# Transposing q and k three loop iterations ahead of their tiles instead of four, with later fills and loads of v

## The chip, the cores and the metric

The kernel runs on one core of a Trainium2 chip. The core has five engines with queues of their own: TensorE (PE, matmuls and transposes), VectorE (DVE), ScalarE (ACT), GpSimd (POOL) and SyncE (SP, which here only issues DMAs). Each engine works through its instructions in order, and waits for others by semaphores. The metric is the time of one execution in microseconds (us).

## What is computed

The program chains three layers; N = 4608 tokens of 512 features come out of the first.

```
scores = scale * q_c @ k_c^T                 # per head and chunk of 64 tokens; B=8, H=8, S=576, D=64
attn   = exp(scores - max) / (sum + 1e-9)
x      = attn @ v_c                          # -> [4608, 512]
e      = argmax(x @ w_gate)                  # one of 8 experts per token
x      = p_e * relu(x @ w1[e]) @ w2[e]       # p_e: the softmax weight of that expert
out    = relu(x @ w_in)**2 @ w_out
```

## The kernel before

The work runs in three stages on the same core: `attention()`, `experts()` and `second()`. The order of the instructions on each engine is the order in which the Python code emits them. Only `attention()` and what stands around it is touched.

Attention works on tiles of 128 tokens (36 tiles, two chunks of 64 each) and loads q and k in units of two tiles (18 units, 512 KB each for q and for k). One loop iteration `it` does, in this order: POOL's `regroup` (L269), a copy of the q or k of a later unit into `by_r`; the `scores` of tile it+1 (PE L311), with DVE's maximum and subtraction (L319, L321); `pv` of tile it-1 (PE L344) with DVE's division (L353 to L356), a store of x, and now and then the load of a later batch's v on POOL's queue (L260); the transposition `ta` of tile it's attention weights (PE L332, copied out by ACT as `aT`, L334); the first half of a transposition of q or k (`trans`, PE L294); `x_t`, a transposition of an older tile's x (PE L371, copied out by DVE L372); the exponential of tile it+1 (ACT L326); and the second half of `trans`. Every fourth iteration the router's steps are added (`gate`, `gate_route`, `place`, `scatter`).

`trans` writes two kinds of buffers. For q, ACT copies each half into `qT` (L297). For k, ACT copies each half, in two pieces, into one of the two buffers `kb` (L302), which hold k in a form with zeros between, filled once at the start (`fill_k`). q and k alternate from iteration to iteration, so a unit takes two iterations: in the kernel before, q of unit u is transposed in iteration 2u-4, k in 2u-3, and the first scores of that unit are emitted in iteration 2u-1:

```
u, h2 = divmod(it + 4, 2)
tr = it + 4 < NTILE
if it + 6 < NTILE:
    regroup(it + 6)
```

For the first unit there is no regroup: PE transposes straight from the loaded tile, in 64-row pieces, and ACT copies them out (L288). v lies in two sets of four buffers `vb`, one set for batches 0, 2, .. and one for 1, 3, ..; around the loaded values stand zeros and a column of ones, written once (`fill_v`). Before the loop, POOL issues half of batch 0's v, fills all four buffers of batch 1 and issues the loads of batch 1; DVE fills those of batch 0 inside iteration -3.

At the end of attention, POOL has two more kinds of work: `scatter`, which writes the tokens' places to memory, and parts of the weights' splitting into two halves (L190, behind an ACT cast, L189). The experts' first tokens are gathered by POOL after the last of these scatters. The gathered tokens are transposed on PE and the first expert matmul (L780) follows.

Of the kernel before, what the change touches and what calls it, by code (L numbers as in the profile page):

```python
# [20 lines left out]
def kernel(ctx, tc, q, k, v, w_gate, w1, w2, w_in, w_out, out):  # L21
    nc = tc.nc
# [4 lines left out]
    NCB = S // CH  # L27
    NPAIR = H // 2
    KD = DM // 128
    NTILE = NT // 128  # L30
# [44 lines left out]
    def tl(tag, shape, dt, name):  # L75
        if tag in fixed:
            ts, n = fixed[tag]
            fixed[tag] = ts, n + 1
            t = ts[n % len(ts)].bitcast(dt)
            k = 1  # L80
            for z in shape[1:]:
                k *= z
            t = t[0:shape[0], 0:k]
            names = "abcde"[:len(shape) - 1]
            return t.rearrange(f"p ({' '.join(names)}) -> p {' '.join(names)}", **dict(zip(names, shape[1:])))
        if tag == "m":

            t = sb.tile([128, 32], F32, tag=tag, name=name, bufs=NBUF[tag]).bitcast(dt)
            names = "abc"[:len(shape) - 1]
            n = 1  # L90
            for z in shape[1:]:
                n *= z
            return t[0:shape[0], 0:n].rearrange(f"p ({' '.join(names)}) -> p {' '.join(names)}", **dict(zip(names, shape[1:])))
        return sb.tile(shape, dt, tag=tag, name=name, bufs=NBUF[tag])
# [134 lines left out]
    def attention():  # L229
        with ExitStack() as actx:  # L230
# [4 lines left out]
            vb = [[tl("hhhhhhba"[4 * s + p], [128, NCB, 2, D + 1], F32, f"vb{s}{p}") for p in range(NPAIR)] for s in range(2)]  # L235
# [5 lines left out]
            def load_qk(u):  # L241
                qk = tl("a", [128, 2, H, 2 * D], F32, f"qk{u}")
                for j, (src, nm) in enumerate(((q, "q"), (k, "k"))):
                    t = qk[:, j]
                    g = 4 * u
                    done = 0
                    while done < 4:
                        b, c = divmod(g + done, NCB)
                        n = min(4 - done, NCB - c)
                        nc.sync.dma_start(  # L250
                            out=t[32 * done:32 * (done + n)],
                            in_=src[b, :, c * CH:(c + n) * CH, :].rearrange("h (p r) d -> p h (r d)", r=2),
                        )
                        done += n
                    st[nm, u] = t

            def load_v(b, engs=(nc.gpsimd,), c0=0, c1=NCB):
                for p in range(NPAIR):
                    for j in range(2):
                        engs[j % len(engs)].dma_start(  # L260
                            out=vb[b % 2][p][64 * j:64 * j + 64, c0:c1, j, 0:D],
                            in_=v[b, 2 * p + j, CH * c0:CH * c1].rearrange("(c s) d -> s c d", s=CH),
                        )

            def regroup(z):
                u, j = divmod(z, 2)
                if u:
                    src = st["qk"[j], u].rearrange("p h (r d) -> p r h d", r=2)
                    nc.gpsimd.tensor_copy(out=by_r[:, z % 4], in_=src)  # L269

            def trans(nm, u, hh):
                if hh == 0:
                    if nm == "q":
                        st["qT", u] = tl("b", [128, NPAIR, 128, 2], F32, f"qT{u}")
                src = st[nm, u] if hh == 0 else st.pop((nm, u))
                ps = ps_t.tile([128, 2, 2, 128], F32, tag="t", name="tq")
                if u == 0:
                    for h in range(4):
                        nc.tensor.transpose(ps[:, h // 2, h % 2, :], src[:, 4 * hh + h, :], ident)
                    for r in range(2):  # L280
                        for j in range(2):
                            i_ = ps[64 * r:64 * r + 64, :, j, :]
                            if nm == "q":
                                o = st["qT", u][64 * j:64 * j + 64, 2 * hh:2 * hh + 2, :, r]
                            else:
                                i_ = i_.rearrange("p a (c i) -> p a c i", c=4)
                                o = kb[u % 2].rearrange("p a c j (i r) -> p a j c i r", r=2)[64 * j:64 * j + 64, 2 * hh:2 * hh + 2, j, :, :, r]
                            nc.scalar.copy(o, i_)  # L288
                    return
                z = 2 * u + (nm == "k")  # L290
                for a in range(2):
                    for r in range(2):
                        h = 4 * hh + 2 * a
                        nc.tensor.transpose(ps[:, a, r, :], by_r[:, z % 4, r, h:h + 2, :].rearrange("p h d -> p (h d)"), ident)  # L294
                i_ = ps.rearrange("p a r i -> p a i r")
                if nm == "q":
                    nc.scalar.copy(st["qT", u][:, 2 * hh:2 * hh + 2], i_)  # L297
                else:
                    o = kb[u % 2].rearrange("p a c j (i r) -> p j a c i r", r=2)
                    i_ = i_.rearrange("p a (c i) r -> p a c i r", c=4)  # L300
                    for j in range(2):
                        nc.scalar.copy(o[64 * j:64 * j + 64, j, 2 * hh:2 * hh + 2], i_[64 * j:64 * j + 64])  # L302
# [21 lines left out]
            def expo(i):  # L324
                at = st["at", i]
                nc.scalar.activation(out=at, in_=at, func=AF.Exp, scale=scale)  # L326

            def attn_t(i):
                at = st.pop(("at", i))
                ps = ps_t.tile([128, NPAIR, 128], F32, tag="t", name="ta")  # L330
                for p in range(NPAIR):
                    nc.tensor.transpose(ps[:, p, :], at[:, 2 * p:2 * p + 2, :], ident)  # L332
                aT = tl("r", [128, NPAIR, 128], F32, "aT")
                nc.scalar.copy(aT, ps)  # L334
                st["aT", i] = aT
# [60 lines left out]
            def fill_k(s):  # L396
                t = kb[s]
                nc.vector.memset(t[0:64, :, :, 1, :], 0.0)
                nc.vector.memset(t[64:128, :, :, 0, :], 0.0)

            def fill_v(s, eng):
                for t in vb[s]:
                    eng.memset(t[0:64, :, 1, :], 0.0)
                    eng.memset(t[64:128, :, 0, :], 0.0)
                    eng.memset(t[0:64, :, 0, D:D + 1], 1.0)
                    eng.memset(t[64:128, :, 1, D:D + 1], 1.0)

            fill_k(0)
            load_qk(1)
            c = min(6, NCB)  # L410
            load_v(0, (nc.gpsimd, nc.sync), 0, c)
            load_qk(2)
            if c < NCB:
                load_v(0, (nc.gpsimd, nc.sync), c)
            fill_v(1, nc.gpsimd)
            load_v(1)

            todo = {}
            for i in range(NTILE - 2):
# [6 lines left out]
            for g in range(NG - 1):  # L426
                t = 4 * g + (7 if g < NG - 3 else 6)
# [9 lines left out]
                    gather_tk(0)  # L437
                    gather(0)

            for it in range(-4, NTILE + 1):  # L440
                u, h2 = divmod(it + 4, 2)
                tr = it + 4 < NTILE
                if it + 6 < NTILE:
                    regroup(it + 6)
                if 0 <= it + 1 < NTILE:
                    scores(it + 1)
                if 0 <= it - 1 < NTILE:
                    pv(it - 1)
                    lo, hi = (2 * (it - 1)) // NCB, (2 * (it - 1) + 2) // NCB
                    if hi > lo and lo + 2 < B:  # L450
                        load_v(lo + 2)
                if 0 <= it < NTILE:
                    attn_t(it)
                if tr:
                    trans("qk"[h2], u, 0)
                for step, i in todo.get(it, ()):
                    step(i)
                if 0 <= it + 1 < NTILE:
                    expo(it + 1)
                if tr:  # L460
                    trans("qk"[h2], u, 1)
                    if h2 == 1 and u + 3 < NUNIT:
                        load_qk(u + 3)
                if it == -4:
                    fill_k(1)
                if it == -3:
                    fill_v(0, nc.vector)
                if it == -1:
                    constants()
                late_steps(it)  # L470
                if it == NTILE - 14:
                    for _ in range(4):
                        load_next(most=1)
                if NTILE - 5 <= it < NTILE - 2:
                    split(1, 0, it - NTILE + 5, eng=nc.gpsimd)
# [599 lines left out]
    with tc.manual_schedule():  # L1075
        attention()
        experts()
        second()
# [30 lines left out]
```

## Time and profile before

| | |
|---|---|
| median of 3 runs | 1463.49 us (1463.39 to 1469.42) |
| the profiled execution | 1463.5 us, of which the span from first to last instruction is 1461.7 us |
| PE busy | 1414.8 us (97%) |
| DVE busy | 766.7 us (52%) |
| ACT busy | 551.6 us (38%) |
| POOL busy | 502.5 us (34%) |
| mean granted PE clock | 0.991 of full speed |

The page lists each engine's busy time over the whole span. Attention is only the first eighth of it, so the stage is read from the busy time in short stretches and from the timeline. In the timeline a row is one instruction or several equal ones in a row (xcount): its start and length in us, the engine, the line of the code, and what it writes from what. In brackets stands how long the engine sat idle before, and who ended that wait.

### The profile page before, as it was taken

What the parts mean: (1) busy time and instruction counts of PE and PEld (TensorE: products, weight loads), DVE (VectorE), ACT (ScalarE), POOL (GpSimd) and SP (SyncE); (2) the same over time, 40 slices, a digit from 0 to 9 for tenths busy, and PEclk for the clock granted to TensorE, in tenths of its full rate; (3) what the DMA queues carried; (4) which work ended last, traced back from release to release, by engine and by line L of the source; (5) the groups of instructions that cost most, each with busy time, mean ns of one, the idle gap of its engine ahead of it and who ended that gap; (6) DMA issues with size and microseconds to landing.
All of it is one profiled execution on the core that took longest, in us unless ns stands there. A gap on an engine that the chain in (4) does not pass through costs nothing.

```text
span 1461.7 us, 21577 instructions
## 1 busy us (share of the span) xinstructions
PE 1414.8 (97%) x8186; PEld 1220.7 (84%) x8186; DVE 766.7 (52%) x1374; ACT 551.6 (38%) x941; POOL 502.5 (34%) x600
## 2 busy tenths in 40 slices
PE   5998889999999999999999999999999999999998
PEld 4887778888889999997888888888888888888886
DVE  4888877578888777884532223323322232232222
ACT  4665534344344446554432222222222222222222
POOL 6665754435555446743003040210404012040201
PEclk8999999999999999999999999999999999999999
DMA  9999546767677778884201010100101001010000
GB/s 206 266 219 255 166 143 188 211 195 231 208 240 234 221 234 262 265 271 155 73 6 55 1 60 0 38 23 1 60 0 60 0 22 38 1 60 0 31 2 29
DMA packets 144369, 172.90 MB, mean 118 GB/s; under 512 B 18160, under 2 KB 103872, under 8 KB 144256
## 3 DMA queue, kind: packets, MB, share of 16 engines
q1 hardware_dynamic: 110032, 112.58, 27.2%
q0 software_dynamic: 17920, 40.51, 9.7%
q10 hardware_dynamic: 16304, 18.36, 3.8%
q8 instruction: 66, 1.08, 0.3%
q14 instruction: 47, 0.39, 0.1%
HBM read 133.05 MB, written 38.34 MB: 117 GB/s over the span
## 4 chain that ended last, share of the span: by engine, by line
PE 54%; POOL 0%; POOLq 0%; issue 0%; DVE 0%
PE hp L1018 27%; PE py L1039 27%; POOL out_dram L999 0%; POOLq L1104 0%; DVE o L1047 0%; POOL between L998 0%
## 5 line engine op out<-in xcount | busy, mean ns | idle before, releaser
L1018 PE MATMUL hp<-xm,w_None 128*128 128x512 f32 x1728 | 416.7, 391 | 3.3 <-DVEq L962 3.3
L1018 PEld LDWEIGHTS hp<-xm,w_None 128*128 128x128 f32 x1728 | 325.5, 188 | 71.5 <-issue 3.5
L1039 PE MATMUL py<-w_None,h 128*128 128x512 f32 x1512 | 363.2, 389 | 0.0
L1039 PEld LDWEIGHTS py<-w_None,h 128*128 128x128 f32 x1512 | 283.9, 188 | 58.8
L1023 DVE SCALAR_TENSOR_TENSOR rs<-hp,rs 128x512 f32<-128x512 f32 x144 | 99.6, 692 | 434.1 <-ACT rs L1022 434.1
L1022 ACT ACTIVATE rs<-hp 128x512 f32<-128x512 f32 x144 | 86.0, 597 | 455.4 <-PE hp L1018 455.3
L999 POOL DMA_INDIRECT out_dram<-o,tp x36 | 35.1, 974 | 628.0 <-ACT o L1045 622.0
L780 PE MATMUL pa<-xs,w 128*128 128x256 f32 (+2 forms) x1344 | 243.8, 331 | 4.9 <-ACT xs L771 2.0
L792 PE MATMUL pb<-h,w 128*128 128x256 f32 (+2 forms) x1344 | 243.9, 331 | 0.0
L780 PEld LDWEIGHTS pa<-xs,w 128*128 128x128 f32 x1344 | 212.9, 191 | 22.6 <-DVE h L784 3.9
L792 PEld LDWEIGHTS pb<-h,w 128*128 128x128 f32 x1344 | 210.0, 190 | 14.4
L1025 DVE TENSOR_TENSOR h<-rs,h 128x512 fp32r<-128x512 f32 x144 | 99.8, 693 | 98.9 <-ACT h L1024 98.2
L190 DVE TENSOR_TENSOR w<-raw,w 128x1024 fp32r<-128x1024 f32 x100 | 134.0, 1341 | 17.2 <-ACT w L189 14.8
L783 ACT ACTIVATE h<-pa 128x256 fp32r<-128x256 f32 (+2 forms) x112 | 53.2, 475 | 219.1 <-PE pa L780 187.9
L1024 ACT CAST h<-rs 128x512 fp32r<-128x512 f32 x144 | 89.4, 621 | 111.5 <-DVE rs L1023 111.5
L189 ACT CAST w<-raw 128x1024 fp32r<-128x1024 f32 x113 | 118.1, 1046 | 0.0
L828 POOL TENSOR_TENSOR cr<-cr 128x256 f32<-128x256 f32 x64 | 49.5, 774 | 125.0 <-ACT h L783 48.0
L784 DVE SCALAR_TENSOR_TENSOR h<-pa,h 128x256 fp32r<-128x256 f32 (+2 forms) x112 | 59.6, 535 | 60.6 <-ACT h L783 57.2
L829 POOL TENSOR_TENSOR cr<-cr 128x256 f32<-128x256 f32 x64 | 73.7, 1151 | 5.0
L294 PE MATMUL tq<-ident,by_r 128*128 128x128 f32 x272 | 41.4, 279 | 14.0 <-POOL by_r L269 14.0
L223 POOL DMA_INDIRECT xg<-x_d,tk x40 | 44.6, 1116 | 28.0 <-PE pt L769 18.1
L1039 PE MATMUL py<-w,h 128*128 128x512 f32 x216 | 51.7, 389 | 0.0
(202 smaller groups left out, 1318.4 us busy)
## 6 DMA issues: line engine op xcount, KB each, us to landing
raw<-in_moe_w_dram SPq DMA_DIRECT2D x112, 512.0 KB, 4.1
x_d<-x SPq DMA_DIRECT2D x36, 256.0 KB, 6.2
x<-y_d POOLq DMA_DIRECT2D x36, 256.0 KB, 3.0
cr<-in_moe_w_in_dram SPq DMA_DIRECT2D x32, 256.0 KB, 4.2
cr<-in_moe_w_out_dram SPq DMA_DIRECT2D x32, 256.0 KB, 5.2
vb<-in_v_dram POOLq DMA_DIRECT2D x56, 144.0 KB, 8.0
qk<-in_q_dram SPq DMA_DIRECT2D x12, 512.0 KB, 8.6
qk<-in_k_dram SPq DMA_DIRECT2D x12, 512.0 KB, 10.7
```

Of the source, the lines that this page charges most:

```text
L189: nc.scalar.copy(w[0], raw)
L190: eng.tensor_tensor(out=w[1], in0=raw, in1=w[0], op=ALU.subtract)
L780: nc.tensor.matmul(ps[:, 0:N], lhsT=w[wl][:, kk, o:o + 128], rhs=xT[:, xl, kk, 0:N], start=(kk == 0 and wl + xl == 0), stop=(kk == KD - 1 ...
L784: nc.vector.scalar_tensor_tensor(out=h[:, 1, 0:N], in0=ps[:, 0:N], scalar=0.0, in1=h[:, 0, 0:N], op0=ALU.max, op1=ALU.subtract)
L792: nc.tensor.matmul(pb[d][:, 0:N], lhsT=w[wl][:, f % 2, 128 * d:128 * d + 128], rhs=h[:, hl, 0:N], start=(f + hl + wl == 0), stop=(f == NF ...
L829: nc.gpsimd.tensor_tensor(out=af, in0=af, in1=ef, op=ALU.add)
L1018: nc.tensor.matmul(ps, lhsT=w[wl][:, kk, o:o + 128], rhs=xT[:, xl, kk, :], start=(kk == 0 and wl + xl == 0), stop=(kk == KD - 1 and wl == 1))
L1022: nc.scalar.activation(out=rs[:, 0], in_=ps, func=AF.Relu)
L1023: nc.vector.scalar_tensor_tensor(out=rs[:, 1], in0=ps, scalar=0.0, in1=rs[:, 0], op0=ALU.max, op1=ALU.mult)
L1024: nc.scalar.copy(h[:, 0], rs[:, 1])
L1025: nc.vector.tensor_tensor(out=h[:, 1], in0=rs[:, 1], in1=h[:, 0], op=ALU.subtract)
L1039: nc.tensor.matmul(ys[t], lhsT=h[:, hl, 128 * t:128 * t + 128], rhs=w[wl][:, g % 2, :], start=(g == 0 and hl + wl == 0), stop=(g == NF2 - ...
```

## The change

`trans` runs one iteration later relative to the tiles: the loop starts at -3, q of unit u is transposed in iteration 2u-3 and k in 2u-2; the scores of the unit's first tile stay in 2u-1. `regroup` stays two iterations ahead of `trans`. Router steps keep their iteration numbers, so that `gate`, which stood in k iterations up to 27, now stands in q iterations. ACT's copies of the first unit's k move to DVE. `fill_v` takes a part of the four buffers: DVE fills two of batch 0 before the loop, POOL the other two; POOL fills batch 1's buffers in two parts, in iterations -2 and 0, and issues their loads in -1 and 0. `constants` moves from iteration -1 to 2. Lines from 258 on shift by up to five.

```diff
--- before.py
+++ after.py
@@ -254,8 +254,8 @@
                         done += n
                     st[nm, u] = t
 
-            def load_v(b, engs=(nc.gpsimd,), c0=0, c1=NCB):
-                for p in range(NPAIR):
+            def load_v(b, engs=(nc.gpsimd,), c0=0, c1=NCB, ps=range(NPAIR)):
+                for p in ps:
                     for j in range(2):
                         engs[j % len(engs)].dma_start(
                             out=vb[b % 2][p][64 * j:64 * j + 64, c0:c1, j, 0:D],
@@ -280,12 +280,14 @@
                     for r in range(2):
                         for j in range(2):
                             i_ = ps[64 * r:64 * r + 64, :, j, :]
+                            eng = nc.scalar.copy
                             if nm == "q":
                                 o = st["qT", u][64 * j:64 * j + 64, 2 * hh:2 * hh + 2, :, r]
                             else:
+                                eng = nc.vector.tensor_copy
                                 i_ = i_.rearrange("p a (c i) -> p a c i", c=4)
                                 o = kb[u % 2].rearrange("p a c j (i r) -> p a j c i r", r=2)[64 * j:64 * j + 64, 2 * hh:2 * hh + 2, j, :, :, r]
-                            nc.scalar.copy(o, i_)
+                            eng(o, i_)
                     return
                 z = 2 * u + (nm == "k")
                 for a in range(2):
@@ -398,22 +400,25 @@
                 nc.vector.memset(t[0:64, :, :, 1, :], 0.0)
                 nc.vector.memset(t[64:128, :, :, 0, :], 0.0)
 
-            def fill_v(s, eng):
-                for t in vb[s]:
+            def fill_v(s, eng, ps):
+                for t in vb[s][ps]:
                     eng.memset(t[0:64, :, 1, :], 0.0)
                     eng.memset(t[64:128, :, 0, :], 0.0)
                     eng.memset(t[0:64, :, 0, D:D + 1], 1.0)
                     eng.memset(t[64:128, :, 1, D:D + 1], 1.0)
 
+            A, Z = slice(0, NPAIR // 2), slice(NPAIR // 2, NPAIR)
+            HA, HZ = range(NPAIR // 2), range(NPAIR // 2, NPAIR)
             fill_k(0)
+            fill_v(0, nc.vector, A)
+            fill_k(1)
             load_qk(1)
             c = min(6, NCB)
             load_v(0, (nc.gpsimd, nc.sync), 0, c)
             load_qk(2)
             if c < NCB:
                 load_v(0, (nc.gpsimd, nc.sync), c)
-            fill_v(1, nc.gpsimd)
-            load_v(1)
+            fill_v(0, nc.gpsimd, Z)
 
             todo = {}
             for i in range(NTILE - 2):
@@ -437,11 +442,15 @@
                     gather_tk(0)
                     gather(0)
 
-            for it in range(-4, NTILE + 1):
-                u, h2 = divmod(it + 4, 2)
-                tr = it + 4 < NTILE
-                if it + 6 < NTILE:
-                    regroup(it + 6)
+            for it in range(-3, NTILE + 1):
+                u, h2 = divmod(it + 3, 2)
+                tr = it + 3 < NTILE
+                if it + 5 < NTILE:
+                    regroup(it + 5)
+                if it in (-2, 0):
+                    fill_v(1, nc.gpsimd, A if it < 0 else Z)
+                if it in (-1, 0):
+                    load_v(1, ps=HA if it < 0 else HZ)
                 if 0 <= it + 1 < NTILE:
                     scores(it + 1)
                 if 0 <= it - 1 < NTILE:
@@ -461,11 +470,7 @@
                     trans("qk"[h2], u, 1)
                     if h2 == 1 and u + 3 < NUNIT:
                         load_qk(u + 3)
-                if it == -4:
-                    fill_k(1)
-                if it == -3:
-                    fill_v(0, nc.vector)
-                if it == -1:
+                if it == 2:
                     constants()
                 late_steps(it)
                 if it == NTILE - 14:
```

On PE, in the first iterations with the full set of steps, this is where the transposes of unit 3's k (`tq_484` is its second half) stood before. kb1 is what they end up in, sc are scores:

```order
L294 MATMUL tq_484<-ident_69,by_r_116 128x128 x4
L311 MATMUL sc_497<-kb0_114,qT2_316 64x128 x8
L344 MATMUL pv_510<-vb00_106,aT_468 64x130 x2
L344 MATMUL pv_510<-vb01_107,aT_468 64x130 x2
L344 MATMUL pv_510<-vb02_108,aT_468 64x130 x2
L344 MATMUL pv_510<-vb03_109,aT_468 64x130 x2
L332 MATMUL ta_525<-ident_69,at_446 128x128 x4
L294 MATMUL tq_533<-ident_69,by_r_116 128x128 x4
L371 MATMUL tx_539<-ident_69,x_410 128x128 x4
L294 MATMUL tq_546<-ident_69,by_r_116 128x128 x4
L311 MATMUL sc_553<-kb1_115,qT3_420 64x128 x8
```

Between them and the scores that read kb1 stand the scores of another tile, pv, ta and a whole transposition of q. The same place after the change, with `tq_526` as the second half of that k:

```order
L334 MATMUL ta_505<-ident_69,at_432 128x128 x4
L296 MATMUL tq_512<-ident_69,by_r_116 128x128 x4
L373 MATMUL tx_519<-ident_69,x_384 128x128 x4
L296 MATMUL tq_526<-ident_69,by_r_116 128x128 x4
L313 MATMUL sc_539<-kb1_115,qT3_456 64x128 x8
L346 MATMUL pv_552<-vb00_106,aT_510 64x130
```

The scores that read kb1 now follow the transposes directly. On ACT, the copies that lie between the two, before:

```order
L334 COPY aT_468<-ta_463 128x512
L302 COPY kb1_115<-tq_470 64x8x64 x2
L326 ACTIVATE at_446<-at_446 128x512
L302 COPY kb1_115<-tq_484 64x8x64 x2
L334 COPY aT_530<-ta_525 128x512
```

and after:

```order
L336 COPY aT_510<-ta_505 128x512
L304 COPY kb1_115<-tq_512 64x8x64 x2
L328 ACTIVATE at_488<-at_488 128x512
L304 COPY kb1_115<-tq_526 64x8x64 x2
L336 COPY aT_580<-ta_575 128x512
```

Their order on ACT is the same: aT, half of kb, the exponential, the other half, and the next tile's aT. On POOL, ahead of the loop and in its first iterations, before the change (vb10 to vb13 are batch 1's buffers, by_r the regrouped q and k; qk1 is unit 1):

```order
L403 MEMSET vb13_113 64x9x65
L404 MEMSET vb13_113 64x9x65
L405 MEMSET vb13_113 64x9
L406 MEMSET vb13_113 64x9
L260 DMA vb10_110<-in_v_dram 64x9x64 x2
L260 DMA vb11_111<-in_v_dram 64x9x64 x2
L260 DMA vb12_112<-in_v_dram 64x9x64 x2
L260 DMA vb13_113<-in_v_dram 64x9x64 x2
L269 COPY by_r_116<-qk1_131 128x1024 x2
L269 COPY by_r_116<-qk2_142 128x1024 x2
```

and after, from the last fill of batch 0's buffers:

```order
L407 MEMSET vb03_109 64x9
L408 MEMSET vb03_109 64x9
L269 COPY by_r_116<-qk1_141 128x1024 x2
L405 MEMSET vb10_110 64x9x65
L406 MEMSET vb10_110 64x9x65
L407 MEMSET vb10_110 64x9
L408 MEMSET vb10_110 64x9
L405 MEMSET vb11_111 64x9x65
L406 MEMSET vb11_111 64x9x65
L407 MEMSET vb11_111 64x9
L408 MEMSET vb11_111 64x9
L269 COPY by_r_116<-qk2_152 128x1024
```

The two copies for unit 1 stood behind four fills and eight loads of batch 1, and now stand ahead of them; the copies for unit 2 stand between the fills and loads.

## Rows read from the trace of the kernel before

**Rows 1.** Busy time of each engine in two stretches; then PE's granted clock, DMA share, GB/s.

```profile
0.00:18.00 18.00, 3.71 (x16) 3.14 (x16) 8.62 (x21) 7.38 (x17) 16.44 (x41) 0.83 1.04 202
...
36.00:54.00 18.00, 18.00 (x233) 16.34 (x232) 13.62 (x28) 12.67 (x24) 12.01 (x14) 1.00 1.12 273
```

**Rows 2.** Timeline, the first 25 us: start, us, engine line op tile xcount [idle <-releaser].

```profile
5.66 0.55 DVE L403 MEMSET vb<- 64x585 f32 x1 [0.16 <-issue]
...
8.19 0.64 POOL L403 MEMSET vb<- 64x585 f32 x1
...
9.52 3.12 ACT L288 COPY kb<-tq 64x256 f32<-64x256 f32 x8
...
11.99 0.07 DVE L406 MEMSET vb<- 64x9 f32 x1
...
14.29 5.85 POOL L260 DMA_DIRECT2D vb<-in_v_dram  x8
...
20.19 4.03 POOL L269 COPY by_r<-qk 128x1024 f32<-128x1024 f32 x4
...
21.27 1.97 PE L294 MATMUL tq<-ident,by_r 128*128 128x128 f32 x8 [12.36 <-POOL by_r L269]
...
23.17 1.98 PE L311 MATMUL sc<-kb,qT 128*64 128x128 f32 x16
```

**Rows 3.** Timeline, a k iteration without routing work (PE, ACT, DVE).

```profile
36.13 1.09 PE L311 MATMUL sc<-kb,qT 128*64 128x128 f32 x16
...
38.80 0.59 ACT L334 COPY aT<-ta 128x512 f32<-128x512 f32 x1 [1.14 <-PE ta L332]
...
39.28 1.17 ACT L302 COPY kb<-tq 64x512 f32<-64x512 f32 x2
...
39.72 0.68 DVE L372 COPY xTs<-tx 128x512 f32<-128x512 f32 x1
...
39.94 1.09 PE L311 MATMUL sc<-kb,qT 128*64 128x128 f32 x16
...
41.13 1.17 ACT L302 COPY kb<-tq 64x512 f32<-64x512 f32 x2
```

**Rows 4.** Timeline, the scores of four iterations that follow each other, 50 to 65 us.

```profile
51.36 1.09 PE L311 MATMUL sc<-kb,qT 128*64 128x128 f32 x16
...
56.17 1.09 PE L311 MATMUL sc<-kb,qT 128*64 128x128 f32 x16
...
60.41 1.09 PE L311 MATMUL sc<-kb,qT 128*64 128x128 f32 x16
...
64.33 1.09 PE L311 MATMUL sc<-kb,qT 128*64 128x128 f32 x16
```

**Rows 5.** Timeline, from the end of attention to the first expert matmul.

```profile
171.18 1.09 PE L311 MATMUL sc<-kb,qT 128*64 128x128 f32 x16
...
171.19 4.68 POOL L190 TENSOR_TENSOR w<-raw,w 128x1024 fp32r<-128x1024 f32 x2 [3.74 <-ACT w L189]
...
172.14 1.04 ACT L189 CAST w<-raw 128x1024 fp32r<-128x1024 f32 x1
...
179.34 2.00 PE L344 MATMUL pv<-vb,aT 128*64 128x130 f32 x16 [3.45 <-DVE x L356]
...
195.35 0.44 PE L780 MATMUL pa<-xs,w 128*128 128x384 f32 x1 [0.68 <-ACT xs L771]
```

**Rows 6.** DMA issues between 3.3 and 5 us: KB, us from issue to landing.

```profile
qk<-in_k_dram SPq DMA_DIRECT2D x1, 512.0 KB, 11.0
```

**Rows 7.** Timeline around a routing step, 95 to 103 us.

```profile
95.41 3.45 DVE L497 TENSOR_TENSOR lc<-lg,lmx 128x32 f32<-128x32 f32 x1
...
95.81 3.00 POOL L269 COPY by_r<-qk 128x1024 f32<-128x1024 f32 x3
...
99.41 0.58 ACT L334 COPY aT<-ta 128x512 f32<-128x512 f32 x1 [4.24 <-DVE ei L501]
...
102.46 1.11 PE L344 MATMUL pv<-vb,aT 128*64 128x130 f32 x16 [1.11 <-DVE x L356]
```

## The prediction

> **What bounds the kernel now.** I read the page's busy shares first (PE 97% of 1461.7 us), then the busy time in stretches of 18 us [rows 1], and then the timeline of the attention stage alone, since every edit lies in it or ahead of it. The rest of the program begins only when attention is over, so what the change does to that end is what it does to the total. Three places matter.
>
> The start: PE transposes q and k of the first unit (two tiles of 128 tokens) by 9 us and then sits idle for 12.36 us until POOL has copied the next q, and the first scores start at 23.17 us [rows 2]. POOL was late because it first filled the four v buffers of batch 1 (8.19 to 14.29) and then issued their eight loads (5.85 us); its four copies begin at 20.19 [rows 2].
>
> The middle: PE is busy for all 18 us of 36 to 54 [rows 1]. A loop iteration without routing work lasts 39.94 - 36.13 = 3.81 us from scores to scores [rows 3], and PE works through it without a gap. One with the gate's matmul lasts 56.17 - 51.36 = 4.81, one with the gate's transposes 4.24, one with the ranks 3.92 [rows 4]: +1.0, +0.43 and +0.11. In the iteration that transposes k (a "k iteration"; the others are "q iterations"), ACT does aT, two copies into kb, the exponential, and two more copies into kb. The last of these ends at 41.13 + 1.17 = 42.30, which is 2.36 us after PE has begun the next iteration's scores [rows 3]. Before the change nobody minds: those scores still read the other unit's kb.
>
> The end: around 171 to 183 us DVE is held up, PE waits 3.45 us for an x, and the first expert matmul starts at 195.35 [rows 5].
>
> **What the change does to the start.** DVE's fills of batch 0 take 5.66 to 12.06 for four tiles [rows 2]; two of them go to POOL, so DVE's fills end near 8.9 us. Then come eight copies of the first k, moved from ACT, where they took 3.12 us [rows 2]. DVE copying such a piece out of PSUM is not shown. The nearest bounds are 2.7 us (half of DVE's full-size copy, 0.68 each [rows 3]) and 5.4 us (the full-size copy eight times); I take ACT's 3.1, so the scores of tile 0 end near 12.4 us instead of 25.2. POOL fills two tiles until 11.3 (half of the 6.1 us in [rows 2]), copies q of unit 1 by 12.3 (4.03 / 4 each) and k of unit 1 once it has landed. That load was issued at 3.38 and landed 11.0 us later, at 14.4 [rows 6]. So that copy ends at 15.4, the transposes of k run until about 17, and ACT's chain of 3.5 us (42.30 - 38.80 [rows 3]) ends near 20.4, which is when the scores of tile 2 can be finished. POOL's later steps (a fill of 3.05, a copy of 1.0 and half the loads, 2.9, twice) end at 30 us. None of them holds up its own iteration by more than 0.5 us. Constants moved to iteration 2 are 1 us of DVE work that nothing awaits before the first routing.
>
> Going on from tile 2: 3.4 us for a q iteration without tx (four transposes, 0.43, less), 5.8 for the k iteration (worked out below), 3.8, 5.8, 3.8, 5.8. The scores that begin iteration 7 then start at 49.0 us; before, they started at 51.36 [rows 4]. Of some 11 us won at the first tile, 2.4 are left there.
>
> At this place the Trainium skill has a rule that speaks against the change: "DMA: Bandwidth & Descriptors", section "Issuing engines are not separate DMA queues", says that loads started by SP and POOL run on the same 16 DMA engines and interleave. The trace agrees, with a share of 1.04 in the first 18 us and 1.12 in 36 to 54 [rows 1]. By that rule postponing v only changes who gets the bandwidth, and the sum would be 1473 plus the up to 4 us of the third rival, which is worked out there from rows.
>
> **What it does to each k iteration.** The lead of three means that k of a unit is transposed in the iteration just before the scores of that unit's first tile. PE's order has those scores directly behind the last transposes. They come as two halves, head pairs 0 and 1 and then 2 and 3, and each half needs its own ACT copies. Measured from the start of a k iteration, the first copies end at 39.28 + 1.17 - 36.13 = 4.32 and the second at 6.17 [rows 3]. The first four score matmuls run in between. The other four start at 6.2 us, as if the scores had begun at 5.8 (four of eight matmuls are 0.4 us). A k iteration becomes 5.8 us instead of 3.81, so 2.0 us are lost on PE. Everything behind the scores on PE's queue (pv, ta, the next transposes) waits too, and DVE's maximum with it. What could cover it: gate transposes (0.43) now fall on k iterations and hide in the wait. The gate's matmul (1.0), which used to share the k iteration, now falls on q iterations and costs in full.
>
> From iteration 7 to 33 that is 13 k iterations at 5.8 (75.5), 13 q iterations at 3.81 (49.5), six gates (6.0), six ranks (0.7) and one gate transpose on a q iteration (0.4): 132 us. Before it was 171.18 - 51.36 = 119.8 [rows 4, 5]. Of those, 26 x 3.81 + 7 x 1.0 + 7 x 0.43 + 6 x 0.11 = 109.8 were PE's own work and 10.0 waits of other kinds. The clearest: DVE's lc, a comparison of two SBUF operands, takes 3.45 us where POOL copies by_r from 95.81 on, ACT's aT waits 4.24 us behind it, and PE 1.11 us for an x [rows 7]. I count these as gone, because PE now waits in every k iteration anyway and DVE and POOL catch up there. So iteration 33 starts at 49.0 + 132.1 = 181.1, which is 9.9 us later than 171.18.
>
> **The end.** The scatter that opens the way to the experts stands on POOL behind two weight splits; before they ran from 171.19 to 175.87 [rows 5]. The second split waits for an ACT cast that now stands behind the last kb copies: 175.3 + 6.2 + 1.0 + 2.3 puts the scatter at 184.9, 8.9 us later than 175.9. A split is 4.68 / 2 and the cast 1.04 [rows 5]; the gathers that the experts need follow on the same engine. PE's own chain gains, since its 3.45 us wait goes; but PE then waits for POOL, perhaps with slower matmuls behind the wait, as at 179.34, where sixteen pv took 2.00 us and at 102.46 1.11 [rows 5, 7]: 0 to 1 us more. Expert start and total: +9 to +10. The profiled execution took 1463.5 us (span 1461.7 and 1.8 around it), the same as the median of 1463.49. Forecast: 1463.5 + 9.5 = 1473.
>
> **The rivals.** *Faster: the copies arrive in time.* Place: the scores behind each k transposition, 17 times. If PE is late there for other reasons, the 2.0 us are hidden. For it: with a gate in the k iteration PE came 1.0 us later [rows 4]. Against it: gates leave the k iterations, and ACT's 3.5 us chain begins only at ta's end, wherever PE stands. Price: a stall of 0.8 instead of 2.0 gives 1473 - 17 x 1.2 = 1453; it decides below 1.0 us per k iteration.
>
> *No change: the waits pay for it.* PE's 3.45 us wait and the slower matmuls behind it go, and POOL's scatter is not what starts the experts: 1473 - 4 = 1469, and a start that is 2 us better gives 1467. For it: before, 10 us of waits between iterations 7 and 33 were not PE work. Against: I have already counted these.
>
> *Slower still: data and collisions.* The second half of batch 1's v is issued by 30 us, and pv of tile 4 needs it at 40. By then five units of q and k (5.2 MB), two batches of v (2.4) and two stores of x (0.5) have to be through, 8.1 MB; at the 202 GB/s of the first stretch [rows 1] that takes 40 us, at 273 less, so it comes 0 to 4 us late. If half the 10 us of collisions comes back, that is 5 more: 1478 to 1482.
>
> **How the numbers follow.** Forecast 0.55 (1469 to 1477), faster 0.05, no change 0.22, slower still 0.18. What a measurement of this kernel can tell from no change is about 0.5%, 7.3 us: 1456.2 to 1470.8. A fifth of the forecast's own range and most of the no-change case lie under 1470.8: together 0.30 within, 0.65 slower, 0.05 faster. The range 1465 to 1481 leaves out the faster case and the far end of the slower one.
>
> **What would show it.** In the profile after: the first scores of tile 0 at 11 to 13 us; POOL's first by_r near 11.3; in each plain k iteration a PE wait of about 1.4 us in the middle of the scores, ended by ACT's kb copy, and 5.8 us from scores to scores; q iterations at 3.81; the scores of tile 34 near 181 and the first expert matmul near 204. The forecast is wrong if the scores do not wait for kb, if k iterations stay under 4.8 us, or if the expert stage starts at the same time though attention ended later.

## The result, and the profile after

The changed kernel takes 1476.42 us (median of 7 runs, 1473.70 to 1478.64), the kernel before 1463.49 in the same comparison: a ratio of 1.0084, interval 1.0066 to 1.0102. It is slower by 12.9 us; the forecast was +9.5, to 1473. The profiled execution took 1476.13 us, with a span of 1473.6 (+11.9).

Busy time in the two stretches of [rows 1], after the change (PE, PEld, DVE, ACT, POOL; then PE's granted clock, DMA share, GB/s):

```profile
0.00:18.00 18.00, 10.56 (x63) 8.54 (x64) 11.57 (x24) 6.02 (x13) 14.25 (x35) 1.00 1.05 200
36.00:54.00 18.00, 14.63 (x184) 12.82 (x181) 10.53 (x23) 9.85 (x19) 10.86 (x13) 1.00 1.10 263
```

PE is busy for 10.56 us of the first 18 instead of 3.71, and then for 14.63 of 18 where it was busy all the time. Some of the busy time at the start is slowness: up to 17.2 us PE's matmuls take about twice as long as later (the sixteen scores at 15.36 below 1.95 us, those at 35.62 1.09), although the clock column gives 1.00 for that stretch. The DMA shares hardly moved. The timeline of the start, against [rows 2]:

```profile
8.77 3.49 DVE L290 COPY kb<-tq 64x256 f32<-64x256 f32 x8
...
11.36 1.03 POOL L269 COPY by_r<-qk 128x1024 f32<-128x1024 f32 x1
12.41 1.12 PE L313 MATMUL sc<-kb,qT 128*64 128x128 f32 x8 [0.64 <-DVE kb L290]
...
15.36 1.95 PE L313 MATMUL sc<-kb,qT 128*64 128x128 f32 x16
...
21.49 0.66 PE L313 MATMUL sc<-kb,qT 128*64 128x128 f32 x8 [1.19 <-ACT kb L304]
...
30.64 1.00 PE L313 MATMUL sc<-kb,qT 128*64 128x128 f32 x8 [1.19 <-ACT kb L304]
31.42 1.95 PE L346 MATMUL pv<-vb,aT 128*64 128x130 f32 x16
...
35.62 1.09 PE L313 MATMUL sc<-kb,qT 128*64 128x128 f32 x16
```

The second half of tile 0's scores runs at 12.41. The halves at 21.49 and 30.64 belong to the first tiles of units 1 and 2 (tiles 2 and 4): each is held by ACT's kb copy. At 31.42 the pv takes 1.95 us instead of 1.06: PE's clock has fallen, as the busy time by stretches shows (same columns as above):

```profile
22.00:30.00 8.00, 6.52 (x84) 5.52 (x80) 5.35 (x18) 4.93 (x9) 7.74 (x16) 1.00 1.18 221
...
31.00:34.00 3.00, 3.00 (x26) 2.66 (x24) 1.90 (x5) 0.00 (x0) 1.49 (x2) 0.50 1.22 200
```

A plain k iteration, against [rows 3], begins at 35.62:

```profile
38.28 0.59 ACT L336 COPY aT<-ta 128x512 f32<-128x512 f32 x1 [1.73 <-PE ta L334]
38.77 1.17 ACT L304 COPY kb<-tq 64x512 f32<-64x512 f32 x2
39.96 0.63 ACT L328 ACTIVATE at<-at 128x512 f32<-128x512 f32 x1
39.99 0.66 PE L313 MATMUL sc<-kb,qT 128*64 128x128 f32 x8 [0.49 <-ACT kb L304]
40.62 1.17 ACT L304 COPY kb<-tq 64x512 f32<-64x512 f32 x2
41.84 0.66 PE L313 MATMUL sc<-kb,qT 128*64 128x128 f32 x8 [1.20 <-ACT kb L304]
...
45.21 1.09 PE L313 MATMUL sc<-kb,qT 128*64 128x128 f32 x16
```

The halves of the scores (eight matmuls each) stand right behind the copies that they read. The second half begins 6.22 us after 35.62. With 0.41 us taken off for the first half, as if the scores had run without a gap, the k iteration lasts 5.81, and the q iteration behind it ends at 45.21, 3.78 later. Together they last 9.59 us, whatever is taken off. The waits of PE, 20 to 192 us (engine, line, waited for: us in all, times, longest), after:

```profile
PE sc L313 <- ACT kb L304: 24.9, 25, 2.1
```

and before:

```profile
PE tq L294 <- POOL by_r L269: 14.0, 2, 12.4
PE pv L344 <- DVE x L356: 7.6, 6, 3.4
```

One kind of wait has replaced two others. The end, against [rows 5]:

```profile
178.87 2.36 POOL L190 TENSOR_TENSOR w<-raw,w 128x1024 fp32r<-128x1024 f32 x1 [4.42 <-ACT w L189]
179.21 2.04 DVE L511 TENSOR_TENSOR cm<-cm,c 128x8 bf16<-128x8 bf16 x1
...
182.68 0.63 ACT L328 ACTIVATE at<-at 128x512 f32<-128x512 f32 x1 [1.03 <-DVE at L323]
...
184.53 1.04 ACT L189 CAST w<-raw 128x1024 fp32r<-128x1024 f32 x1
184.56 1.12 PE L313 MATMUL sc<-kb,qT 128*64 128x128 f32 x8 [2.11 <-ACT kb L304]
185.65 2.35 POOL L190 TENSOR_TENSOR w<-raw,w 128x1024 fp32r<-128x1024 f32 x1 [4.42 <-ACT w L189]
188.19 0.99 POOL L540 DMA_INDIRECT tk_d<-tok,pos  x1 [0.15 <-issue]
...
202.42 0.66 PE L774 MATMUL pt<-ident,xg 128*128 128x128 f32 x4 [1.94 <-DMA xg<-x_d,tk]
...
206.47 0.44 PE L785 MATMUL pa<-xs,w 128*128 128x384 f32 x1 [0.68 <-ACT xs L776]
```

The second split waits for an ACT cast behind the last kb copies, the scatter follows it, and PE waits for the gathered tokens. The first expert matmul starts at 206.47 instead of 195.35: +11.1 of the span's +11.9.

### The profile page after: what moved, and what is told of

It is laid out like the page before. It is cut to its first block, busy times and chain, and to the rows that moved or that the text cites. A ratio compares the mean times of both kernels' runs of the same rounds, so it can differ in the third digit from the quotient of the medians.

```text
span 1473.6 us, 21557 instructions
## 1 busy us (share of the span) xinstructions
PE 1419.5 (96%) x8186; PEld 1221.9 (83%) x8186; DVE 761.5 (52%) x1374; ACT 548.7 (37%) x933; POOL 510.1 (35%) x608
## 4 chain that ended last, share of the span: by engine, by line
PE 53%; issue 0%; POOL 0%; POOLq 0%; DVE 0%
PE hp L1023 27%; PE py L1044 26%; POOL out_dram L1004 0%; POOLq L1109 0%; DVE o L1052 0%; POOL between L1003 0%
## 5 line engine op out<-in xcount | busy, mean ns | idle before, releaser
L797 PEld LDWEIGHTS pb<-h,w 128*128 128x128 f32 x1344 | 209.9, 190 | 14.5
L190 DVE TENSOR_TENSOR w<-raw,w 128x1024 fp32r<-128x1024 f32 x100 | 132.0, 1320 | 17.2 <-ACT w L189 13.9
L313 PE MATMUL sc<-kb,qT 128*64 128x128 f32 x576 | 46.0, 294 | 28.4 <-ACT kb L304 25.8
L313 PEld LDWEIGHTS sc<-kb,qT 128*64 128x64 f32 x576 | 32.2, 142 | 44.3 <-ACT kb L304 34.6
```

Source lines behind the costliest of these rows:

```text
L190: eng.tensor_tensor(out=w[1], in0=raw, in1=w[0], op=ALU.subtract)
L313: nc.tensor.matmul(ps[64 * c2:64 * c2 + 64, 2 * p:2 * p + 2, :], lhsT=qt[:, p, 32 * c:32 * c + 32, :].rearrange("p i r -> p (i r)"), rhs=k ...
L797: nc.tensor.matmul(pb[d][:, 0:N], lhsT=w[wl][:, f % 2, 128 * d:128 * d + 128], rhs=h[:, hl, 0:N], start=(f + hl + wl == 0), stop=(f == NF ...
```

## The experiments

The theory: the time goes into PE's wait for ACT's second pair of kb copies, 2 us in each k iteration, and what the new order wins at the start is smaller. Rival 1: the later fills and loads of v cost it. Rival 2: DVE's copies of the first k, or the clock at the start. All ratios are to the kernel before, with 95% intervals. The last columns are from the profiles: the start of the scores of tiles 8 and 34 (of the second half less 0.4, where they are split) and of the first expert matmul.

| kernel | us | ratio | tile 8 | tile 34 | experts |
|---|---|---|---|---|---|
| before | 1463.5 | 1 | 51.4 | 171.2 | 195.4 |
| after | 1476.4 | 1.0066 to 1.0102 | 51.0 | 184.2 | 206.5 |
| lead of four, rest as after | 1462.5 | 0.999 to 1.0008 | 50.8 | 170.6 | 195.8 |
| lead of three alone | 1484.9 | 1.0136 to 1.0168 | 58.8 | 191.9 | 214.4 |
| first k copied by ACT | 1477.8 | 1.0083 to 1.0116 | 50.8 | 184.0 | 206.5 |
| k copies ahead of exp | 1464.5 | 1.0001 to 1.0019 | 47.2 | 171.0 | 194.8 |
| scores behind pv and ta | 1462.0 | 0.998 to 0.9999 | 47.7 | 172.2 | 194.0 |
| half of the k copies on DVE | 1472.9 | 1.0048 to 1.0072 | 47.8 | 182.6 | 203.3 |
| k before q | 1458.1 | 0.9948 to 0.9975 | 45.2 | 166.8 | 189.3 |
| k before q, q copies ahead of exp | 1459.7 | 0.9952 to 0.9979 | 45.1 | 166.7 | 191.0 |

**The lead put back to four.** The loop runs from -4, with all else as after (the fills and loads of batch 1's v are kept behind the same regroup copies).

```diff
-for it in range(-3, NTILE + 1):
+for it in range(-4, NTILE + 1):
-    u, h2 = divmod(it + 3, 2)
+    u, h2 = divmod(it + 4, 2)
-    if it in (-2, 0):
+    if it in (-3, -1):
         fill_v(1, ...)
-    if it in (-1, 0):
+    if it in (-2, -1):
         load_v(1, ...)
```

(`tr` and `regroup` follow, and `constants` moves from 2 to 1.)

> The changed kernel with one thing put back: q and k are transposed four iterations ahead again; DVE's copies of the first k, the smaller fills on GpSimd and the later loads of the second batch's v stay. Theory (the loss is TensorE's wait for ScalarE's second pair of k copies, about 2 us in each k iteration, and the new order at the start is a gain): no wait of scores on ScalarE's k copies in the steady state, scores of tile 0 near 14 us, iterations at 3.8 us; 7 to 10 us under the kernel before, 1453 to 1457 us. Rival 1 (the later fills and loads of v cost the time): stays above 1470 us. Rival 2 (DVE's copies of the first k, or the clock of the start, cost it): not under 1463 us.

1462.52 us: the 12.9 us are gone, and with them the waits of scores for kb. So rival 1 falls as a cause of the loss. Rival 2 misses its own figure, not under 1463 us, by half a microsecond only; the next two runs decide on it. And the gain of 7 to 10 us that I expected from the new start is not there. POOL's row and PE's row near 31 us say why:

```profile
27.80 2.91 POOL L260 DMA_DIRECT2D vb<-in_v_dram  x4
30.75 2.03 POOL L269 COPY by_r<-qk 128x1024 f32<-128x1024 f32 x2
```

```profile
31.85 1.97 PE L296 MATMUL tq<-ident,by_r 128*128 128x128 f32 x8 [3.33 <-POOL by_r L269]
```

Scores of tile 0 begin at 14.35 instead of 23.17, but the copies of unit 3 then stand behind v's fills and loads on POOL, PE waits 3.33 us for them, and its matmuls behind that take twice as long (eight transposes 1.97 us, against 1.04 to 1.09 before the wait). At tile 8 all but 0.6 us of the early start is gone.

**The lead of three alone**, on the kernel before.

```diff
-for it in range(-4, NTILE + 1):
+for it in range(-3, NTILE + 1):
-    u, h2 = divmod(it + 4, 2)
+    u, h2 = divmod(it + 3, 2)
```

(`tr` and `regroup` follow; `fill_k`, `fill_v` and `constants` move by one iteration with the start of the loop.)

> The kernel before with one thing changed: q and k are transposed three iterations ahead; fills, loads and the copies of the first k stay as before. Theory: the wait of about 2 us in each k iteration is there in full, and little of the start is gained since GpSimd's fills still hold up the regrouping copies: 1477 to 1484 us, and scores wait on ScalarE's k copies for 22 us or more between 20 and 180 us. Rival 1 (the later fills and loads of v cost the time): 1462 to 1466 us. Rival 2: 1463 to 1467 us.

1484.90 us, 0.9 above the expected range: the shorter lead by itself costs 21.6 us, with neither the later v nor DVE's copies of the first k in the kernel. Its k iterations last 5.8 us, as in the changed kernel. PE's waits, from 20 to 200 us since attention ends later here:

```profile
PE sc L311 <- ACT kb L302: 25.4, 25, 2.1
PE tq L294 <- POOL by_r L269: 7.4, 1, 7.4
```

The rest of the change wins 8.5 us back if the lead is three (PE's wait of 7.4 us for POOL's copy is not there in the changed kernel), and nothing that can be measured if it is four. The parts don't add up one by one.

**The first unit's k copied by ACT**, as before the change.

```diff
-                                eng = nc.vector.tensor_copy
```

> The changed kernel, in which ScalarE, not VectorE, copies the first unit's k. Theory: the scores of tile 0 end some 2 to 3 us later, and since the first tiles wait for GpSimd's regrouping copies and ScalarE's k copies, less than that is left at tile 8: 1476 to 1479 us. Rival (VectorE's copies of the first k cost time, since they hold up VectorE's fills or stand in the clock's way): under 1474 us.

1477.77 us, as expected, with an interval that overlaps that of the changed kernel. But the first scores come only 0.3 us later, not 2 to 3 (12.70 against 12.41 for the second half), and tile 8 starts no later. Which engine copies the first k is worth nothing that can be measured here, and the loss is there without DVE's copies, as in the run before. So DVE's copies fall as a cause. The clock at the start falls too: with the lead of four the mean granted clock from 30 to 38 us was 0.57, a longer slow stretch than the changed kernel's 31 to 34, and the loss was gone.

**The second k copies ahead of the exponential.**

```diff
+if tr and h2 == 1:
+    trans("k", u, 1)
 if 0 <= it + 1 < NTILE:
     expo(it + 1)
+if tr and h2 == 0:
+    trans("q", u, 1)
 if tr:
-    trans("qk"[h2], u, 1)
```

> The changed kernel, in which ScalarE makes the second pair of k copies ahead of the exponential, not behind it. Theory (the last k copy sets the start of the second half of the scores): that copy ends one exponential, 0.63 us, earlier in each of some 16 k iterations, so 9 to 10 us less than the changed kernel, 1466 to 1468 us; the exponential ends one pair of copies later, and TensorE needs it only after the scores. If the exponential then is what TensorE waits for, the gain is under 4 us (1473 to 1476). Rivals 1 and 2: no change, 1475 to 1477 us.

1464.53 us, 11.9 less than the changed kernel, some 2 us more than the sum. PE's wait for kb halves (20 to 192 us):

```profile
PE sc L313 <- ACT kb L304: 12.7, 24, 0.9
```

A pair of iterations without the gate's matmul takes 42.00 - 33.07 = 8.93 us where the changed kernel takes 45.21 - 35.62 = 9.59: a difference of 0.66 us, about one exponential (0.63). Over 17 pairs that makes 11 us, but the 11.9 are not made of that alone. Tile 2 already starts 1.5 us earlier, in part because PE's matmuls are fast sooner (the sixteen scores at 15.36 take 1.15 us, not 1.95), and PE's clock stays at 1.00 from 31 to 34 us. The halves of tile 34's scores are 1.10 us apart instead of 2.77. Against that, PE waits 3.8 us for DVE's x.

**The scores of a unit's first tile behind pv and ta.**

```diff
-if 0 <= it + 1 < NTILE:
+if 0 <= it + 1 < NTILE and (it < 1 or it % 2 == 0):
     scores(it + 1)
 ...
     attn_t(it)
+if 0 < it and it + 1 < NTILE and it % 2 == 1:
+    scores(it + 1)
```

> The changed kernel, in which TensorE's scores of a unit's first tile are issued behind the product with v and the transposes of the weights of the tiles before, not ahead of them. Theory: the wait is filled by 1.0 to 1.4 us of other matmuls in each of some 16 k iterations: 16 to 22 us less than the changed kernel, 1454 to 1460 us. If the later scores make the exponential and the next transposes late, half of it is paid back: 1464 to 1468 us. Rivals 1 and 2: no change, 1475 to 1477 us.

1461.97 us, 14.5 less: between the two expectations, so neither number held. The wait for kb is filled. In exchange PE waits for DVE's x (5.2 us) and for gathered tokens (3.4), and the experts then begin with the granted clock at 0.50 from 193 to 199 us.

**One of the two k copies on DVE.**

```diff
-nc.scalar.copy(o[64 * j:64 * j + 64, j, 2 * hh:2 * hh + 2], ...)
+(nc.scalar.copy, nc.vector.tensor_copy)[j](o[64 * j:64 * j + 64, j, 2 * hh:2 * hh + 2], ...)
```

> The changed kernel, in which VectorE makes one of the two k copies of each half, ScalarE the other. Theory (the loss is the time that ScalarE needs for four k copies of 0.58 us around its exponential): the last copy ends up to 1.17 us earlier in each of some 17 k iterations, 14 to 20 us less than the changed kernel, 1456 to 1462 us. If VectorE, behind its own maxima, subtractions and divisions, becomes the late one: 1468 to 1476 us, and scores wait on VectorE's k copies. If the loss lay in the fills, loads or the start: no change, 1475 to 1477 us.

1472.85 us, 3.6 less: the theory's number was wrong, the alternative's right. A k iteration:

```profile
65.45 0.69 DVE L358 TENSOR_TENSOR x<-pv,rc 128x512 f32<-128x512 f32 x1
66.10 0.57 ACT L304 COPY kb<-tq 64x512 f32<-64x512 f32 x1
66.18 0.69 DVE L304 COPY kb<-tq 64x512 f32<-64x512 f32 x1
66.90 0.69 DVE L374 COPY xTs<-tx 128x512 f32<-128x512 f32 x1
67.62 0.69 DVE L304 COPY kb<-tq 64x512 f32<-64x512 f32 x1
68.37 0.66 PE L313 MATMUL sc<-kb,qT 128*64 128x128 f32 x8 [0.79 <-DVE kb L304]
```

ACT is done at 66.67. DVE's second copy ends at 68.31, since x and xTs (and the maximum and subtraction before them) stand ahead of its copies on DVE. From 20 to 192 us the scores wait 21.9 us for DVE's copies, against 24.9 for ACT's in the changed kernel. Half the work on a second engine has not halved the wait, since that engine has a queue too.

**k before q.** q and k change places everywhere; nothing is added. Then ACT's q copies, one of 0.59 us for each half, stand ahead of the unit's first scores, and kb has one iteration more.

```diff
-for j, (src, nm) in enumerate(((q, "q"), (k, "k"))):
+for j, (src, nm) in enumerate(((k, "k"), (q, "q"))):
-z = 2 * u + (nm == "k")
+z = 2 * u + (nm == "q")
-trans("qk"[h2], u, 0)
+trans("kq"[h2], u, 0)
```

(and the same exchange in `regroup` and in the second `trans`.)

> The changed kernel with q and k exchanged: k of a unit is regrouped, loaded and transposed an iteration ahead of its q, so that what stands right ahead of a unit's first scores is ScalarE's q copy (one of 0.59 us a half), not its k copies (two of 0.58 us). Nothing is added or taken out. Theory: the last copy ends 1.17 us earlier, 14 to 20 us less than the changed kernel, 1456 to 1462 us. If the length of the queue ahead (weights' copy, exponential) and not the k copies makes the wait: under 6 us less, 1470 to 1476 us.

1458.06 us: 18.4 less than the changed kernel, as expected, and 0.25% to 0.52% under the kernel before, so it beats both. PE's waits, 20 to 192 us:

```profile
PE pv L346 <- DVE x L358: 7.1, 6, 2.4
PE sc L313 <- ACT qT L299: 3.4, 10, 0.5
```

The wait for copies is down from 24.9 to 3.4 us; the waits for DVE's x that the kernel before had (7.6) are back. Of the 18.4 us, 5.8 are won by tile 8.

**k before q, and the second q copy ahead of the exponential.**

```diff
+if tr and h2 == 1:
+    trans("q", u, 1)
 if 0 <= it + 1 < NTILE:
     expo(it + 1)
+if tr and h2 == 0:
+    trans("k", u, 1)
 if tr:
-    trans("kq"[h2], u, 1)
```

(against the kernel with k before q.)

> The changed kernel with q and k exchanged, and ScalarE makes the second q copy ahead of the exponential. Theory: 1.17 and 0.63 us of the 2.0 us of wait go, in some 17 iterations: 29 us by the sum; some 8 to 12 of it come back as the waits that stood in the kernel before too (GpSimd blocking VectorE, q and k not loaded yet in the first tiles), so 1452 to 1459 us, under the kernel before. If the other waits take back all that is over the kernel before: 1461 to 1464 us.

1459.66 us, not to be told from the last one, and 0.7 above the expected range. The wait for q copies falls from 3.4 to 0.5 us, and the wait for DVE's x rises from 7.1 to 10.2: what one wait gave, the other took.

**Two ways to issue v's later loads**, with k before q: in two iterations, or half of them by SyncE.

```diff
     if hi > lo and lo + 2 < B:
-        load_v(lo + 2)
+        load_v(lo + 2, ps=HA)
+        rest.append(lo + 2)
+    elif rest:
+        load_v(rest.pop(), ps=HZ)
```

(`rest` is a list, empty before the loop.)

```diff
-load_v(lo + 2)
+load_v(lo + 2, (nc.gpsimd, nc.sync))
```

> The changed kernel with q and k exchanged, and GpSimd issues the eight loads of a later batch's v in two iterations, four in each, not all in one. Theory on what is left over in the kernel with q and k exchanged (six stops of TensorE, 7.1 us in all, in which a comparison of VectorE of 0.19 us takes 1.6 to 3.1 us beside two or three of GpSimd's regrouping copies that have piled up behind v's loads and the scatter): with a pause among the loads fewer copies pile up and 3 to 6 us of it go, 1452 to 1456 us. If the pile-up comes from the scatter alone: no change, 1457 to 1460 us.

> The changed kernel with q and k exchanged, and half of the loads of each later batch's v are issued by SyncE, half by GpSimd, not all by GpSimd. Theory as for the loads in two iterations: GpSimd is free 3 us earlier in each of six places, its copies no longer pile up, 1452 to 1456 us. If SyncE's queue, waiting for the buffer of v, holds back the stores of x or the loads of q and k behind it: 1458 to 1464 us, with regrouping copies that wait longer for q and k.

1468.15 and 1468.84 us, on another chip on which the kernel before took 1473.01: ratios 0.9959 to 0.9989 and 0.9956 to 0.9985, intervals that overlap that of k before q alone (0.9948 to 0.9975). So the 3 to 6 us more that I expected are not there. With SyncE's help the wait for DVE's x does fall, from 7.1 to 2.6 us, but POOL's regroup copies now wait 33 us for q and k between 36 and 190 us (21.9 for k, 11.1 for q; with k before q alone 10.8 and 0.7). In two iterations the wait for x is 4.5 us, and the copies wait 18.9 (11.6 and 7.3). k before q alone was not run on this chip, so how much of these differences is the chip's is open.

## Why the prediction was right, and where it was off

**The main step held.** A k iteration of 5.8 us (measured 5.81), a q iteration of 3.81 (3.78), a wait of about 1.4 us in the middle of the scores (1.20, and 0.49 ahead of the first half), ended by ACT's kb copies. The prediction speaks of four of eight matmuls; the rows show eight of sixteen, and the 0.4 us that it takes for them is close all the same: a pair of iterations lasts 9.59 us against 9.61. From tile 8 to tile 34: 133.1 us against 132.1 worked out and 119.8 before; the 1.0 between is the last k iteration, which lasted 6.8. Undoing the lead takes the loss away, moving one exponential behind the copies takes 0.66 us from a pair of iterations, and putting the shorter copy last takes nearly all of the wait for copies. Three of the prediction's sums are off in the last digit (48.8 for 49.0, 109.7 for 109.8, 184.8 for 184.9), which changes nothing.

**The 10 us of other waits did go, but what made them did not.** PE's waits for x fell from 7.6 us between 20 and 192 us to none that the view lists. DVE's two lc instructions still met POOL's copies, for less time. Before (line, engine, what, count, busy us and mean ns of one, idle before):

```profile
L498 DVE SCALAR_TENSOR_TENSOR lc<-lc,io 128x32 f32<-128x32 f32 (+1 forms) x8 | 7.0, 869 | 0.3
L497 DVE TENSOR_TENSOR lc<-lg,lmx 128x32 f32<-128x32 f32 (+1 forms) x8 | 5.9, 744 | 0.8
```

After:

```profile
L503 DVE SCALAR_TENSOR_TENSOR lc<-lc,io 128x32 f32<-128x32 f32 (+1 forms) x8 | 4.1, 515 | 0.3
L502 DVE TENSOR_TENSOR lc<-lg,lmx 128x32 f32<-128x32 f32 (+1 forms) x8 | 2.5, 312 | 0.8
```

Undisturbed, one takes 0.19 us, 3 us for the sixteen. So the blocking fell from some 10 us to some 3.5 (the longest lc from 3.52 to 1.92 us), and PE's own wait hid most of what was left. In the variants that take PE's wait for copies away, waits for x are back: 7.9 us with the lead of four, 7.1 and 10.2 with k before q, 5.2 with the scores behind pv and ta. The Trainium skill states a mechanism in "SBUF — State Buffer", section "Who interferes with whom": a VectorE instruction with two inputs in SBUF contends with a GpSimd instruction that reads SBUF, and issue order decides which of the two blocks. The trace agrees on the first part: lc beside by_r's copies [rows 7], and cm, 2.04 us instead of 0.17, beside the split at 178.87. On the order it agrees for cm, which began behind the split; lc's row in [rows 7] begins 0.40 us ahead of the copies' row, so the trace does not show it there.

**The start was mis-sized.** The sum left 2.4 us of the early start at the scores of tile 8 (49.0 against 51.36). Measured: 51.0, so 0.3. The step that failed is "Going on from tile 2", 3.4, 5.8, 3.8 us and so on. Counted back from 49.0, it puts tile 4 at 29.8 and tile 5 at 33.6. Tile 4 came at 30.2 (30.64 - 0.41), tile 5 at 35.62: the q iteration between took 5.4 us and not 3.8. PE ran at 0.50 of its clock from 31 to 34 us, right behind two waits of 0.92 and 1.19 us, and did its matmuls at half speed. The 0.4 us at tile 4 come from before tile 2: the transposes of unit 1's k ended at 18.8 us and not at 17, since the transposes and scores ahead of them ran slowly. The prediction had a term for slow matmuls behind a wait at the end, and none at the start, where the same waits are and where its own [rows 2] show slow ones (sixteen scores in 1.98 us). In runs where the two waits were shorter (0.92 and 0.54 us with the k copies ahead of the exponential, 0.51 and 0.34 with k before q), PE stayed at 1.00 from 31 to 34 us. No run isolates what makes the clock fall.

**The end was right in kind, and 2 us short.** Splits, scatter and gathers did set the experts' start. The scatter came at 188.19 against 184.9: 2 us are those of the start, 1 us is cm, blocked by the first split, which delayed the exponential (1.03 us of wait at 182.68) and with it the last kb copies. From the scatter to the first expert matmul it then took 18.3 us, against 19.2 before, so 0.9 us of this came back.

**The rivals.** "Faster": ten of the 13 k iterations between tiles 8 and 34 lasted 5.8 us, the others 5.9 to 6.8. "No change": POOL's chain does start the experts. "Slower still": no late v is to be seen (no row in which pv waits for vb's load), so its 0 to 4 us did not come. Of its other half, collisions that come back, only the one with cm in the last k iteration shows in PE's time. The prediction also took from the Trainium skill ("DMA: Bandwidth & Descriptors", section "Issuing engines are not separate DMA queues") that loads of all issuing engines share 16 DMA engines. Shares of 1.05 and 1.10 against 1.04 and 1.12 do not speak against it, and who got the bandwidth cost nothing visible.

## What to carry to other kernels

A lead over several iterations is not only there for the engine that fills the buffer: count the copies that stand between producer and consumer in the evicting engine's queue, with all that stands ahead of them. Where two operands need copies of different length, make the longer one first and put the shorter right ahead of its use: against the changed kernel that won 18 us here without an instruction more or less. A gain at the start that rests on one engine's order can be taken back by the next thing in that engine's queue, as with the lead of four here, so follow it for several tiles before counting it.

## What the runs showed of the hardware

PE's granted clock went to 0.50 (1.2 GHz of 2.4) in the midst of work, from 31 to 34 us, after 8 us at 1.00 with PE busy for 6.52 of them and two waits of about 1 us; in the steady state waits of 0.49 and 1.20 us in each k iteration left it at 1.00. DVE copied the 64x256 pieces of k out of PSUM in 0.44 us each (3.49 for eight), against ACT's 0.39, and the 64x512 pieces in 0.69 against 0.58. The kernel before took 1463 us on one chip and 1473 on another.
